# RWKV6 attention followed by an MLP on one core: the second MLP product of one more round in three one-pass products, with a new order of the work

## The chip, the cores and the metric

The kernel runs on one core of a Trainium2 chip. The metric is the device time in microseconds from launch to end, given as the median of several runs; a profile of one further execution shows where the time goes. TensorE (PE) does matrix products, VectorE (DVE), ScalarE (ACT) and GpSimd (POOL) do elementwise work, and SyncE (SP) issues nearly all DMAs.

## The reference

Inputs r, k, v, w are (4, 8, 768, 48) in fp32, u is (8, 48). The attention is a recurrence over 768 steps with a 48 x 48 state per batch and head:

```
for t in range(S):
    cur = einsum('bhd,bhe->bhde', u * kt, vt)
    y[:, :, t] = einsum('bhd,bhde->bhe', rt, state + cur)
    state = wt[:, :, :, None] * state + einsum('bhd,bhe->bhde', kt, vt)
```

Its output is laid out as x of (4, 768, 384), and the MLP block follows, with w_ch1 of (384, 1536) and w_ch2 of (1536, 384):

```
xn = (x - mu) / sqrt(var + 1e-06) * g_ln
out = x + maximum(xn @ w_ch1, 0) @ w_ch2
```

## The kernel before

**Rounds.** The work is cut into eight rounds: four batches by two halves of 384 steps. A round has a *front* (the attention) and a *back* (normalisation and MLP).

**Front.** Inputs are loaded (`nat_w`, `nat_k`, `nat_r`, `v`), multiplied up inside groups of four steps (`inner`), transposed on PE (`k_ps`, `r_ps`, `w_ps`) and copied out by ACT. The steps of a chunk of 64 are then combined over doubling distances: at each level PE multiplies r with k (`quads`, `a<-r,k` in the profile), and DVE scales k and r by products of w (`grow`, the in-place products `k<-k,tot` and `r<-r,tot`). When k is fully scaled, PE transposes it back (`kn_ps`), forms key-value products (`a<-v,k`), and DVE runs the state over the chunks (`s`, `last`). PE adds the part inside a chunk (`a<-v,A`) and the part from the state (`a<-s,r`), and x is copied out.

**Back.** DVE takes statistics (`stats`, `mv`), xn is made and transposed (`xT_ps`, `xf`). The first product has 12 blocks f of 128 hidden columns. In round 0 it is done in plain fp32, where one matmul goes through the array several times (two records in the profile). In rounds 1 to 7 (`THREE = 1`) xn and w_ch1 are split into a high part H, a low part L and a mixed part D, stored as fp32r, and three one-pass products give the same sum: `go_d` with D, a scaling in place by ACT (`shrink`), then `go` with L and H. H is made by ACT, L by DVE or POOL, D by DVE. The D part of w_ch1 lies in DRAM and is streamed in blocks (`d<-w1d`) into 32 homes.

**Second product.** There are two forms, and the number `LAST` decides. Rounds below `LAST` use plain fp32: for each of three tiles of 128 steps, 12 matmuls of 128 x 384 into one bank (`o<-ffn,h`), issued three at a time, and one DVE addition into x. Rounds from `LAST` on use `thirds`: ACT makes the H part of each h block, DVE or POOL the L part, DVE the D part, and for each f and tile three one-pass matmuls follow. The outputs lie in the two `a` banks (tiles 0 and 1) and in `o_2P` and `o_2D` (tile 2); two DVE additions per tile, scaled by `rstd` and `rstdD`, bring them into x, and each tile is stored by itself. Before, `LAST = NR - 4`, so rounds 4 to 7 use `thirds`.

**Where the parts of w_ch2 lie.** `halve2` makes the H, L and D parts of the second weight once. They go into the homes that the fronts use for k, r, A, nat_k, nat_r, v, vx and tot (`w2_place`). They can be written only when the last front no longer needs those homes; besides, the first matmul of a `thirds` round names x of the last round as needed:

```
if first:
    need += x_of(NR - 1)
```

So x of every round from `LAST` on is kept until then. Tile x has three homes, the last round's x lies in the home of `nat_w`.

**The order.** Each piece of work is an operation of the class `Plan` with a cost, what it needs, and the homes it takes. The table `ORDER` lists the operations in the order in which they are recorded; an entry above 10000 names the second or third engine where there is a choice. Each engine runs its instructions in that order. Where the planner expects PE to wait over 0.35 us it puts *fillers* in front, matmuls of zeros named `idle`, which write a free bank. All instructions are recorded by one helper, so every row of the profile has line 47, and tiles are the way to tell them apart.

Of the kernel before, what the change touches and what calls it, by code (L numbers as in the profile page):

```python
# [63 lines left out]
class Plan:  # L64
# [12 lines left out]
        2, 3, 10, 5, 14, 4, 12, 13, 8, 9, 265, 11, 16, 263, 260, 7, 18, 17, 19, 10015, 22, 10020, 264,  # L77
        10021, 25, 262, 27, 261, 23, 6, 24, 29, 266, 269, 267, 110, 268, 26, 128, 30, 270, 273, 271, 28,
        275, 112, 113, 42, 111, 272, 36, 122, 130, 276, 281, 98, 282, 283, 129, 131, 124, 10277, 278,
        65, 37, 38, 288, 274, 132, 43, 44, 10292, 10031, 123, 284, 289, 290, 286, 134, 35, 457, 279,  # L80
        291, 99, 45, 463, 287, 133, 10285, 140, 460, 39, 46, 47, 48, 49, 303, 32, 280, 136, 125, 50,
        10293, 126, 10053, 135, 100, 102, 306, 114, 305, 101, 464, 459, 127, 304, 458, 307, 297, 465,
        462, 461, 310, 308, 51, 311, 309, 10033, 312, 52, 103, 10034, 316, 54, 10294, 152, 313, 317,
        137, 296, 41, 142, 143, 433, 314, 315, 318, 411, 57, 60, 468, 55, 58, 63, 141, 59, 10323, 319,
        320, 116, 299, 321, 322, 56, 138, 466, 467, 139, 298, 470, 324, 327, 64, 69, 40, 70, 325, 469,
        10471, 10295, 330, 92, 66, 62, 61, 67, 117, 118, 68, 73, 328, 332, 473, 326, 104, 119, 329, 333,
        331, 475, 120, 338, 476, 71, 105, 340, 472, 72, 74, 75, 106, 78, 76, 77, 107, 79, 339, 10477,
        336, 344, 337, 10080, 81, 82, 300, 342, 0, 10085, 1, 482, 302, 301, 88, 90, 483, 10478, 91, 334,
        10474, 484, 146, 335, 345, 341, 89, 343, 485, 94, 86, 492, 488, 10095, 121, 144, 115, 87, 486,
        494, 493, 346, 347, 652, 348, 350, 349, 489, 154, 495, 353, 487, 490, 244, 246, 10496, 351, 93,  # L90
        354, 479, 242, 355, 158, 352, 153, 491, 145, 10497, 148, 147, 357, 356, 10498, 509, 10155, 358,
        243, 245, 10361, 247, 10362, 481, 510, 511, 248, 654, 164, 655, 365, 367, 96, 480, 156, 108,
        434, 249, 159, 366, 160, 149, 252, 250, 368, 109, 176, 363, 157, 97, 150, 162, 251, 364, 513,
        383, 658, 165, 653, 10161, 182, 413, 163, 384, 178, 166, 375, 167, 253, 240, 381, 373, 382, 236,
        10179, 177, 657, 376, 656, 183, 515, 514, 151, 516, 414, 660, 212, 369, 662, 241, 517, 435, 184,
        237, 10666, 659, 421, 664, 512, 663, 180, 214, 370, 425, 200, 501, 518, 500, 502, 503, 374, 387,
        10520, 385, 519, 170, 661, 521, 377, 254, 668, 171, 522, 504, 172, 173, 174, 386, 665, 378, 379,
        536, 505, 215, 506, 534, 168, 255, 670, 388, 185, 669, 532, 10499, 10671, 674, 258, 188, 535,
        533, 259, 10672, 850, 530, 528, 531, 10673, 10419, 380, 507, 256, 202, 10667, 83, 540, 213, 541,
        257, 529, 508, 524, 423, 389, 437, 201, 679, 391, 390, 537, 206, 525, 194, 675, 683, 424, 181,  # L100
        680, 527, 526, 449, 189, 676, 392, 10429, 238, 239, 684, 681, 538, 542, 371, 687, 203, 539, 677,
        682, 196, 847, 10439, 192, 543, 523, 10197, 689, 544, 169, 175, 412, 216, 218, 195, 372, 546,
        545, 198, 224, 547, 549, 436, 199, 688, 685, 204, 853, 851, 359, 550, 190, 551, 686, 690, 409,
        548, 220, 678, 10191, 186, 230, 207, 422, 205, 849, 426, 187, 193, 698, 552, 696, 697, 852, 417,
        410, 431, 210, 554, 360, 403, 10691, 398, 430, 219, 208, 225, 232, 848, 854, 695, 553, 222, 427,
        418, 555, 221, 10559, 209, 226, 704, 10233, 84, 707, 399, 706, 705, 228, 857, 404, 211, 393,
        855, 420, 699, 708, 441, 709, 10560, 231, 10558, 415, 217, 566, 234, 235, 710, 692, 856, 858,
        567, 394, 571, 428, 701, 416, 227, 229, 223, 10693, 700, 442, 572, 556, 395, 568, 712, 714, 573,
        10715, 859, 574, 432, 400, 557, 561, 562, 576, 405, 694, 713, 861, 401, 711, 10863, 406, 716,
        396, 703, 402, 575, 438, 601, 586, 591, 563, 860, 569, 564, 450, 443, 565, 570, 602, 407, 603,  # L110
        10864, 592, 440, 577, 578, 593, 397, 702, 717, 604, 447, 579, 723, 869, 720, 605, 580, 722,
        10865, 587, 725, 594, 724, 588, 726, 866, 731, 581, 870, 867, 10868, 595, 589, 727, 874, 582,
        721, 728, 732, 876, 590, 719, 871, 718, 729, 444, 10862, 877, 737, 596, 611, 448, 583, 730, 875,
        733, 872, 10455, 882, 597, 606, 738, 1045, 873, 883, 598, 1042, 584, 878, 880, 734, 1048, 445,
        881, 879, 599, 10453, 585, 607, 884, 735, 1047, 616, 1044, 741, 446, 646, 451, 608, 885, 742,
        736, 617, 10743, 600, 612, 456, 1043, 1050, 1049, 739, 452, 740, 10886, 899, 744, 618, 1046,
        901, 613, 10745, 1053, 1052, 900, 10746, 747, 1054, 619, 620, 454, 1055, 609, 614, 615, 11051,
        647, 903, 621, 748, 626, 622, 610, 1058, 890, 631, 1056, 636, 623, 11057, 893, 811, 891, 892,
        627, 887, 749, 904, 1060, 750, 1061, 905, 624, 816, 637, 625, 902, 10888, 894, 628, 632, 771,
        896, 638, 907, 10754, 1059, 633, 895, 1064, 10755, 634, 635, 909, 11062, 910, 906, 629, 648,  # L120
        908, 911, 1069, 776, 926, 1066, 630, 649, 1065, 753, 766, 1070, 639, 1063, 898, 912, 408, 650,
        922, 767, 768, 924, 917, 923, 806, 1071, 756, 925, 897, 757, 640, 10769, 1228, 1222, 1077, 1078,
        751, 641, 1072, 1073, 761, 1075, 762, 758, 1076, 914, 10759, 10889, 642, 1074, 1225, 763, 916,
        920, 1223, 1088, 1229, 918, 921, 643, 1226, 1230, 913, 770, 919, 10764, 1067, 644, 1085, 796,
        765, 760, 915, 1079, 1224, 777, 927, 1068, 1086, 1227, 1232, 645, 1231, 11236, 11237, 812, 1087,
        826, 1080, 807, 813, 1234, 778, 808, 928, 929, 781, 1094, 809, 814, 1096, 1097, 1233, 1095, 810,
        797, 11081, 1238, 1235, 11240, 798, 815, 779, 817, 930, 1098, 782, 786, 791, 799, 1101, 780,
        818, 783, 784, 787, 934, 788, 1100, 1089, 931, 1239, 932, 801, 789, 935, 11241, 11082, 790,
        1244, 819, 827, 11242, 933, 821, 939, 820, 936, 800, 1246, 828, 785, 1249, 792, 829, 802, 1091,
        1243, 10937, 1245, 1099, 1320, 1121, 1323, 1090, 10938, 1250, 830, 793, 1317, 1102, 1253, 1083,  # L130
        1084, 10940, 1092, 772, 794, 941, 1254, 1322, 1265, 803, 773, 795, 1103, 1319, 942, 1266, 944,
        1251, 804, 943, 1104, 1255, 1252, 1105, 1256, 1001, 1318, 1106, 1259, 1247, 1260, 1108, 1107,
        1109, 1325, 774, 822, 1093, 805, 945, 1257, 775, 1267, 1321, 1324, 1248, 823, 946, 1119, 1115,
        1268, 824, 1258, 966, 1269, 1326, 1327, 948, 1116, 1120, 825, 10949, 11329, 1122, 981, 950,
        1021, 1112, 1328, 1331, 11333, 836, 1334, 651, 1110, 1111, 1117, 1113, 1114, 831, 1123, 1274,
        1275, 752, 951, 952, 1330, 953, 1118, 832, 837, 1124, 11335, 961, 956, 1261, 957, 838, 841,
        11336, 839, 958, 842, 1276, 959, 1277, 954, 1339, 962, 11337, 1127, 1125, 1128, 1131, 1344, 843,
        833, 1338, 1332, 1341, 1340, 960, 1132, 1126, 11133, 1272, 1129, 1271, 1278, 1130, 1134, 840,
        11135, 1412, 1360, 1418, 1352, 1415, 971, 834, 955, 963, 1270, 1353, 1136, 10964, 1346, 835,
        1262, 1279, 965, 1345, 1419, 1280, 844, 1413, 1011, 1022, 1016, 1350, 1347, 1351, 1282, 1263,  # L140
        1416, 1362, 1301, 1414, 845, 1420, 1354, 1012, 1137, 1138, 1139, 1355, 947, 1285, 1281, 1284,
        1283, 1002, 1013, 1417, 1348, 1423, 1003, 1023, 1349, 1014, 1024, 1025, 982, 1015, 1004, 967,
        1017, 1286, 11422, 11424, 1005, 11425, 11421, 986, 991, 1302, 1273, 1369, 1006, 1207, 996, 1363,
        1140, 1018, 983, 1287, 1428, 1288, 1141, 1290, 1264, 1426, 1019, 1361, 1372, 976, 1289, 968,
# [1676 lines left out]
```

## Time and profile before

| | |
|---|---|
| median of 3 runs | 476.72 us (476.5 to 477.76) |
| the profiled execution, its own time | 480.65 us |
| its span, first to last instruction | 478.9 us |
| mean granted TensorE clock | 0.991 |
| DMA: moved, mean rate | 56.22 MB, 117 GB/s |

In the profile a row of a group gives the operation, output and inputs by the program's names (buffer numbers left out), sizes, the count, the busy time, the mean length of one, and the idle time in front of it with what ended it. PEld is the weight load, which overlaps the matmuls. A matmul's record is longer than its distance to the next one, since they are pipelined: the distance is what counts in a sum. The granted clock is 1.00 at full speed.

### The profile page before, as it was taken

Reading aid. Unit: us, or ns where it says so; the run is one execution under the profiler, and the core shown is the slowest. Engines: PE = TensorE matmul, PEld = TensorE weight load, DVE = VectorE, ACT = ScalarE, POOL = GpSimd, SP = SyncE. Lnnn points to the kernel's source line nnn. Section 1 sums busy time; section 2 is a strip of 40 time slices with the busy share of each in tenths; the row PEclk is TensorE's granted clock in tenths of the full one; section 3 lists DMA queues with packets and bytes.
Section 4 is the critical chain, followed back from the end, with each engine's and each line's share of the span. In section 5 each row is a group of like instructions: output and inputs, shape, how many; then the busy total and the mean of one; then the engine's idle time right before and its main releaser. Section 6 shows DMA issues by size and latency. Waiting matters only on the chain. (4 is left out here: it accounts for less than half of the span.)

```text
span 478.9 us, 17278 instructions
## 1 busy us (share of the span) xinstructions
PE 465.8 (97%) x7390; PEld 396.4 (83%) x7390; DVE 349.1 (73%) x734; ACT 259.6 (54%) x595; POOL 117.2 (24%) x125
## 2 busy tenths in 40 slices
PE   8998999999989999999999999999999999999996
PEld 4667989766878778996679986779999999999996
DVE  6999999999938766895957986793986543533454
ACT  6786889653842255364215664357683764453530
POOL 3126019013601213603315201000342122102012
PEclk9999999999997999999999999999999999999999
DMA  7985685677265463276186125116231221341001
GB/s 213 262 212 133 196 182 159 187 175 182 70 185 125 117 177 89 65 161 163 23 214 174 25 54 108 30 50 164 83 102 38 86 73 35 103 129 35 26 24 66
DMA packets 105468, 56.22 MB, mean 117 GB/s; under 512 B 61872, under 2 KB 102320, under 8 KB 105392
## 3 DMA queue, kind: packets, MB, share of 16 engines
q1 hardware_dynamic: 105120, 54.92, 44.3%
q8 instruction: 58, 0.95, 0.8%
q14 instruction: 18, 0.15, 0.1%
q10 hardware_dynamic: 272, 0.20, 0.1%
HBM read 45.27 MB, written 7.47 MB: 110 GB/s over the span
## 5 line engine op out<-in xcount | busy, mean ns | idle before, releaser
L47 PE MATMUL o<-ffn,h 128*128 128x384 f32 x288 | 99.8, 489 | 0.0
L47 ACT ACTIVATE h<-h_ps 128x384 f32<-128x384 f32 (+2 forms) x108 | 47.2, 454 | 64.1 <-PE h_ps L47 61.0
L47 PEld LDWEIGHTS o<-ffn,h 128*128 128x128 f32 x288 | 52.3, 190 | 29.1 <-issue 0.2
L47 ACT ACTIVATE h_ps<-h_ps 128x384 f32<-128x384 f32 x84 | 39.1, 478 | 36.6 <-PE h_ps L47 35.7
L47 DVE SCALAR_TENSOR_TENSOR hD<-hH,hL 128x384 fp32r<-128x384 f32 x48 | 26.5, 569 | 35.9 <-POOL hL L47 16.6
L47 PEld LDWEIGHTS a<-r,k 48*56 48x56 f32 (+3 forms) x3072 | 40.1, 123 | 11.9 <-issue 5.8
L47 PE MATMUL h_ps<-xd,d 128*128 128x384 f32 x204 | 48.2, 343 | 0.0
L47 PE MATMUL a<-r,k 48*56 48x32 f32 (+3 forms) x3072 | 44.2, 209 | 3.0 <-issue 2.1
L47 POOL TENSOR_TENSOR hL<-h,hH 128x384 fp32r<-128x384 f32 x22 | 26.2, 1198 | 82.5 <-PE o_2D L47 21.3
L47 PE MATMUL h_ps<-xhl,wl 128*128 128x384 f32 x180 | 42.7, 347 | 0.0
L47 PE MATMUL h_ps<-xhl,wh 128*128 128x384 f32 x180 | 40.1, 333 | 0.0
L47 DVE TENSOR_TENSOR r<-r,tot 112x768 f32<-112x768 f32 (+1 forms) x40 | 32.2, 808 | 9.5 <-PE a L47 9.5
L47 PEld LDWEIGHTS h_ps<-xd,d 128*128 128x128 f32 x204 | 34.3, 189 | 2.7 <-issue 0.3
L47 DVE TENSOR_TENSOR k<-k,tot 112x768 f32<-112x768 f32 (+1 forms) x40 | 31.5, 790 | 6.5 <-PE a L47 5.8
L47 PEld LDWEIGHTS h_ps<-xhl,wh 128*128 128x128 f32 x180 | 31.8, 194 | 0.0
L47 PEld LDWEIGHTS h_ps<-xhl,wl 128*128 128x128 f32 x180 | 31.0, 196 | 0.9 <-ACT h_ps L47 0.2
L47 ACT COPY A<-a 32x384 f32<-32x384 f32 (+5 forms) x60 | 25.0, 424 | 11.3 <-PE a L47 7.1
L47 ACT ACTIVATE hH<-h 128x384 fp32r<-128x384 f32 x48 | 24.1, 518 | 12.4 <-PE a L47 8.7
L47 ACT ACTIVATE xf<-xT_ps,g_sb 128x384 f32<-128x384 f32 (+2 forms) x27 | 14.6, 545 | 24.1 <-PE xT_ps L47 22.3
L47 PE MATMUL h_ps<-xf,w 128*128 128x128 f32 (+1 forms) x144 | 26.2, 332 | 0.0
L47 PE MATMUL idle<-nought 128*128 128x384 f32 (+2 forms) x74 | 24.5, 455 | 0.9 <-DVE eps L47 0.9
L47 DVE TENSOR_TENSOR hL<-h,hH 128x384 fp32r<-128x384 f32 x26 | 14.9, 585 | 14.0 <-PE o_2P L47 5.7
(183 smaller groups left out, 1071.0 us busy)
## 6 DMA issues: line engine op xcount, KB each, us to landing
d<-w1d SPq DMA_DIRECT2D x84, 192.0 KB, 3.0
raw<-in_moe_w_ch_dram SPq DMA_DIRECT2D x24, 384.0 KB, 4.3
nat_w<-in_w_dram SPq DMA_DIRECT2D x24, 192.0 KB, 3.7
nat_r<-in_r_dram SPq DMA_DIRECT2D x24, 192.0 KB, 3.8
v<-in_v_dram SPq DMA_DIRECT2D x24, 192.0 KB, 4.3
nat_k<-in_k_dram SPq DMA_DIRECT2D x23, 192.0 KB, 4.0
w1d<-w1diff SPq DMA_DIRECT2D x12, 192.0 KB, 3.4
out_dram<-x SPq DMA_DIRECT2D x4, 576.0 KB, 4.2
```

The source lines that it names most:

```text
L47: ins = self.tc.keep_in_program_order(f(*args, **kw))
```

## The change

Two numbers and a table change. `LAST` becomes `NR - 5`, so rounds 3 to 7 have their second product as `thirds`, and only rounds 0 to 2 in plain fp32. Rounds above `LAST` put the split parts of xn by turns into two sets of homes (`x_places`), and which round uses which set shifts by one. Tile x gets a fourth home. `ORDER` is replaced as a whole: 2,190 entries instead of 2,124, in a different order from the first entry on, with different choices between DVE, ACT and POOL. The order was searched under random instruction fetches.

```diff
     ORDER = [
-        2, 3, 10, 5, 14, 4, 12, 13, 8, 9, 265, 11, 16, 263, 260, 7, 18, 17, 19, 10015, 22, 10020, 264,
+        10008, 3, 2, 10012, 4, 9, 10, 5, 11, 16, 264, 261, 7, 14, 13, 18, 10019, 262, 17, 265, 260, 263,
...
     HOMES = {
         "nw": 1, "nk": 1, "nr": 1, "pk": 1, "pr": 1, "w4": 1, "vals": 2, "va": 2,
         "k": 2, "r": 2, "tot": 1, "decay": 3, "rk": 1,
-        "v": 1, "vx": 1, "s": 2, "last": 3, "x": 3, "xn": 3,
+        "v": 1, "vx": 1, "s": 2, "last": 3, "x": 4, "xn": 3,
...
     BY = {"DVE": DVE, "POOL": POOL}
     EITHER = ("DVE", "POOL")
-    THREE, LAST = 1, NR - 4
+    THREE, LAST = 1, NR - 5
```

In instructions, 36 plain fp32 matmuls of 128 x 384 go and 108 one-pass matmuls come; DVE has 742 instructions instead of 734, ACT 608 instead of 595, POOL 141 instead of 125, SP 316 instead of 314. The fillers are 45 instead of 37. The first matmul of a second product in one-pass form stood behind 3,728 matmuls of the program and now stands behind 3,589; the first hD stood behind 608 DVE instructions and now stands behind 581.

252 rows, old and new, of the table ORDER are left out of this document.

## The prediction

> **What bounds the kernel now.** I began with the totals on the page of the profile, then cut the span into stretches with the busy time of each engine, then read the groups by cost. The total says that TensorE (PE) is nearly always busy and no other engine comes close:
>
> ```profile
> span 478.9 us, 17278 instructions
> PE 465.8 (97%) x7390; PEld 396.4 (83%) x7390; DVE 349.1 (73%) x734; ACT 259.6 (54%) x595; POOL 117.2 (24%) x125
> ```
>
> An average over stages can hide a second limit, so here is busy time by stretch. The columns are the stretch, its length, then PE, PEld, DVE, ACT and POOL with their counts, the granted clock and the DMA share:
>
> ```profile
> 0.00:50.00 50.00, 45.03 (x812) 32.44 (x813) 46.23 (x121) 38.13 (x87) 16.16 (x33) 1.00 0.75 198
> 50.00:120.00 70.00, 69.98 (x1327) 54.92 (x1326) 68.87 (x136) 48.80 (x120) 19.53 (x16) 1.00 0.71 184
> 120.00:140.00 20.00, 18.89 (x351) 16.79 (x351) 14.23 (x36) 13.71 (x32) 7.79 (x7) 1.00 0.51 144
> 140.00:150.00 10.00, 8.63 (x149) 8.31 (x141) 5.93 (x9) 1.77 (x4) 2.00 (x3) 0.66 0.41 105
> 150.00:348.00 198.00, 197.69 (x4004) 160.41 (x4003) 148.83 (x309) 96.10 (x215) 44.19 (x44) 1.00 0.44 106
> 348.00:474.00 126.00, 125.21 (x770) 123.48 (x769) 63.16 (x124) 61.04 (x142) 27.48 (x23) 1.00 0.20 61
> ```
>
> Three regimes stand here. Up to 120 us VectorE (DVE) is full, 46.23 of 50 and then 68.87 of 70 us, and PE is kept going beside it. From 150 to 348 us PE alone is full (197.69 of 198) and DVE has a quarter of its time free. From 348 us on, the one-pass second products of rounds 4 to 7 run, and PE is full again while DVE works half the time. From about 50 us on, then, work taken off PE shortens the kernel, as long as DVE can deliver sooner what PE needs.
>
> **The main term: the second product of round 3.** The old form is timed where 24 records of it stand in a row (two records make one matmul), up to the start of the next instruction; the new form where 18 one-pass matmuls do in the chain that ended last:
>
> ```profile
> 228.12 7.91 PE L47 MATMUL o<-ffn,h 128*128 128x384 f32 x24
> 235.96 0.25 PE L47 MATMUL a<-v,A 64*64 64x48 f32 x1
> ```
>
> ```profile
> 468.06 2.92 PE a L47 x18
> 470.99 0.16 PE o_2D L47
> ```
>
> Twelve old matmuls take 235.96 - 228.12 = 7.84 us, 0.653 each; 36 of them make a round, 23.5 us. One new matmul takes (470.99 - 468.06) / 18 = 0.163 us; a round has 12 x 3 x 3 = 108, 17.5 us (the mean group rows are longer since neighbouring records overlap). The term is -6.0 us. The weight loads stay hidden: in the stretch from 348 us they run 123.48 of 126 us beside matmuls that lose only 0.79. If that cover went, the price would be bounded by the same 0.79 of 126 us, under 0.2 us for this round.
>
> **What the new form adds on other engines.** Twelve times a high, a low and a difference part of h, six additions into x instead of three, and three stores instead of one:
>
> ```profile
> L47 DVE SCALAR_TENSOR_TENSOR hD<-hH,hL 128x384 fp32r<-128x384 f32 x48 | 26.5, 569 | 35.9 <-POOL hL L47 16.6 <-PE a L47 10.6 <-PE o_2P L47 6.4
> L47 POOL TENSOR_TENSOR hL<-h,hH 128x384 fp32r<-128x384 f32 x22 | 26.2, 1198 | 82.5 <-PE o_2D L47 21.3 <-PE h_ps L47 17.6 <-ACT h_ps L47 10.2
> L47 ACT ACTIVATE hH<-h 128x384 fp32r<-128x384 f32 x48 | 24.1, 518 | 12.4 <-PE a L47 8.7 <-PE o_2D L47 1.5 <-PE o_2P L47 1.3
> L47 DVE TENSOR_TENSOR hL<-h,hH 128x384 fp32r<-128x384 f32 x26 | 14.9, 585 | 14.0 <-PE o_2P L47 5.7 <-ACT hH L47 3.9 <-issue 1.8
> L47 DVE SCALAR_TENSOR_TENSOR x<-a,rstdD,x 128x384 f32<-128x384 f32 x8 | 4.8, 613 | 8.1 <-PE a L47 8.1
> ```
>
> The order gives DVE 12 more hD (12 x 0.569 = 6.8 us), 6 more hL (6 x 0.585 = 3.5) and three more additions (3 x 0.613 = 1.8): 12.1 us. POOL gets 6 hL (6 x 1.198 = 7.2) and ACT 12 hH (12 x 0.518 = 6.2). All of it falls in the last regime, where DVE is busy 63.16, ACT 61.04 and POOL 27.48 of 126 us, so I cost it at nothing. The three smaller stores of round 3 go to SP's queue; behind a store that waits for its addition stand later loads of weight pieces, which have 32 homes to run ahead in, so this too is nothing. The last additions and stores of round 7 are unchanged, and so is the tail.
>
> **What moves.** The parts of the second weight can be made only when every front is done, because they lie in the fronts' homes. Round 3's second product therefore leaves the middle and joins the last regime. On PE, in the middle of the program before, four-pass triples (o3 is round 3's output tile) fill time between pieces of the fronts of rounds 6 and 7:
>
> ```order
> L47 MATMUL a0_66<-r6_4071,k6_4038 32x32 x48
> L47 MATMUL o3_2_4630<-ffn2_6_1439,h3_6_4431 128x384
> L47 MATMUL o3_2_4630<-ffn2_7_1700,h3_7_4251 128x384
> L47 MATMUL o3_2_4630<-ffn2_8_1413,h3_8_4642 128x384
> L47 MATMUL o3_0_4832<-ffn2_3_1146,h3_3_4377 128x384
> L47 MATMUL o3_0_4832<-ffn2_4_1474,h3_4_4395 128x384
> L47 MATMUL o3_0_4832<-ffn2_5_1612,h3_5_4659 128x384
> L47 MATMUL k_ps7_1_4922<-ident_80,pad_k_71 112x128 x4
> L47 MATMUL r_ps7_2_4927<-ident_80,pad_r_72 112x128 x4
> ```
>
> On PE after, the first such work stands behind all fronts, next to round 4's first product (a0 and a1 are output banks, the letter in w2D and hD names the part):
>
> ```order
> L47 MATMUL h_ps4_1_5622<-xk4_4982,wh0_1_1218 128x384
> L47 MATMUL h_ps4_1_5622<-xr4_4983,wh0_2_1037 128x384
> L47 MATMUL a0_66<-w2D0_5340,hD3_0_5606 128x384
> L47 MATMUL a0_66<-w2L0_5334,hL3_0_5491 128x384
> L47 MATMUL a0_66<-w2H0_4969,hH3_0_5263 128x384
> L47 MATMUL a1_67<-w2D0_5340,hD3_0_5606 128x384
> L47 MATMUL a1_67<-w2L0_5334,hL3_0_5491 128x384
> L47 MATMUL a1_67<-w2H0_4969,hH3_0_5263 128x384
> ```
>
> Counting ahead of the first hD matmul: the 36 old matmuls are gone (-23.5 us) and so is a round's worth of first-product matmuls (129 of rounds 4 and 5 before, 21 after: 108 x 0.163 = 17.5 us). PE has 41 us less to fill the front with. DVE loses less there: 581 instructions ahead of its first hD instead of 608. At the 150 to 348 us stretch's mean, 148.83 / 309 = 0.48 us, that is 13 us. So the middle asks DVE for 148.8 - 13.0 = 135.8 us of work in 198 - 41 + 3.5 (next term) = 160.5 us, a share of 85% instead of 75%. Between 50 and 120 us it runs at 98% while PE misses 0.02 us, so 85% can be done; but each place where PE waits for DVE has a shorter cover. The nearest row for such a wait:
>
> ```profile
> PE kn_ps L47 <- DVE k L47: 1.1, 1, 1.1
> ```
>
> Bounds: nothing, since at 98% PE lost nothing, and several such waits, 6 us or more (the second rival). I take one, +1.1 us. The fourth home for x eases one thing: the first outputs of round 6 need the home of round 2 instead of round 3, whose product ends much earlier; I cost it at nothing, as no row shows a wait for it.
>
> **The opening.** On PE at the end of the opening before, the last fillers (idle matmuls, put where the planner expects PE to wait) stand ahead of round 0's first transposes of xn:
>
> ```order
> L47 MATMUL kn_ps0_1_0_697<-ident_80,k0_211 128x112 x4
> L47 MATMUL idle_702<-nought_76 128x384
> L47 MATMUL idle_702<-nought_76 128x128
> L47 MATMUL a0_66<-v0_258,k0_211 48x48 x16
> L47 MATMUL a1_67<-v0_258,k0_211 48x48 x16
> L47 MATMUL w_ps1_0_748<-ident_80,w4_73 112x128 x3
> L47 MATMUL idle_754<-nought_76 128x128
> L47 MATMUL xT_ps0_1_0_756<-ident_80,xn0_0_745 128x128
> ```
>
> On PE after, fillers stand on both sides of those transposes, up to the first first-product matmul:
>
> ```order
> L47 MATMUL idle_896<-nought_76 128x128
> L47 MATMUL xT_ps0_2_0_898<-ident_80,xn0_0_891 128x128
> L47 MATMUL w_ps1_0_903<-ident_80,w4_73 112x128 x3
> L47 MATMUL k_ps1_1_907<-ident_80,pad_k_71 112x128 x4
> L47 MATMUL xT_ps0_0_0_919<-ident_80,xn0_0_891 128x128
> L47 MATMUL xT_ps0_1_0_921<-ident_80,xn0_0_891 128x128
> L47 MATMUL a0_66<-s1_647,r0_210 64x48 x16
> L47 MATMUL idle_943<-nought_76 128x128
> L47 MATMUL a1_67<-r1_802,k1_872 60x32 x48
> L47 MATMUL h_ps0_3_0_995<-xf0_0_941,w1_1_0_107 128x128
> ```
>
> In all there are 45 fillers instead of 37, with 12,416 columns instead of 10,368, and the single filler that stood in the middle is gone.
>
> ```profile
> L47 PE MATMUL idle<-nought 128*128 128x384 f32 (+2 forms) x74 | 24.5, 455 | 0.9 <-DVE eps L47 0.9
> ```
>
> At that row's 24.5 us for 10,368 columns, 2,048 more cost 4.8 us; at the 0.653 us per 384 columns of the warm rows, 3.5 us; if they only fill waits that PE has anyway, nothing. What is not done while DVE paces the opening must be done later on a full PE, so I take +3.5 us.
>
> **A stall and a slow clock.** The stretch 140 to 150 us has a mean granted clock of 0.66. Finer, with the PE instruction at its start:
>
> ```profile
> 141.93 1.30 PE L47 MATMUL a<-r,k 48*60 48x32 f32 x49 [1.37 <-issue]
> ...
> 140.00:142.00 2.00, 0.63 (x44) 0.52 (x39) 0.00 (x0) 0.00 (x0) 0.59 (x2) 1.00 0.19 52
> 142.00:144.00 2.00, 2.00 (x86) 2.00 (x88) 0.63 (x1) 0.67 (x1) 0.00 (x0) 0.55 0.07 20
> 144.00:146.00 2.00, 2.00 (x18) 1.91 (x13) 1.79 (x4) 0.00 (x0) 0.00 (x0) 0.50 0.61 192
> 146.00:148.00 2.00, 2.00 (x8) 2.00 (x7) 1.97 (x4) 1.05 (x2) 0.36 (x1) 0.50 0.65 143
> 148.00:150.00 2.00, 2.00 (x9) 1.88 (x9) 1.53 (x3) 0.05 (x1) 1.05 (x1) 0.74 0.53 118
> ```
>
> PE stands for 1.37 us amid small matmuls and waits for nothing that the profile shows (issue), and then its clock is down over the four stretches of 2 us that follow: 2 x (0.45 + 0.50 + 0.50 + 0.26) = 3.4 us lost. Together 4.8 us. The order after puts other instructions at every such place, so the pair may be gone (-4.8), stay (0) or come twice (+4.8). I take half of its going, -2.4 us, because the plain runs have a median 3.9 us under the profiled one and may not have it each time.
>
> The Trainium skill, page "TensorE: Matmul & The Clock Gate", section "Why this matters for your kernels", says that the clock drops after idle gaps above about 3 us between matmul bursts. By that rule a gap of 1.4 us would cost only itself, the term would be half of 1.4, and the sum below -2.1 instead of -3.8. The trace differs: here 1.37 us among small matmuls was enough.
>
> **The sum.** -6.0 + 3.5 + 1.1 - 2.4 = -3.8 us. The profiled execution takes 480.65 us (span 478.9 and 1.75 around it) and would take 476.9. The shown runs have a median of 476.72; the same difference gives 472.9. About 0.3%, 1.43 us, is what a measurement of this kernel can tell from no change.
>
> **The rivals.**
>
> Nothing left over: the saving is eaten where DVE paces the kernel. The opening costs 4.8 us, plain runs never had the slow clock, and one wait on DVE stays: -6.0 + 4.8 + 1.1 = -0.1 us, 476.6. For it: DVE is full in the opening and the fillers were raised by a fifth. Against: PE's saving is certain work, and most fillers lie where PE waits anyway. Chance 0.20.
>
> Slower: DVE becomes the bound of the middle. The place is the transposes of k (kn_ps) and the quads of rounds 4 to 7, which wait for DVE's scaling of k and r, with 41 us less filler beside them. If DVE gets only to 80% there, halfway between today's 75 and the needed 85, its 135.8 us take 169.8 instead of 160.5: +9.3. In place of the 1.1 the sum is -4.9 + 9.3 = +4.4, 481.1. It decides (1.43 us slower) from 6.3 us of loss, a share of 135.8 / 166.8 = 81%. For it: the order after gives POOL more work, 141 instructions instead of 125, and DVE instructions are seen at twice their length:
>
> ```profile
> L47 DVE SCALAR_TENSOR_TENSOR hD<-hH,hL x48: 523/557/1300, 348.0 to 470.1; 128x384 fp32r<-128x384 f32 x48
> ```
>
> Against: the 98% above. Chance 0.20. The Trainium skill, "GPSIMD Engine Reference", section "Specifications", says that POOL shares its SBUF interfaces with VectorE and contends with DVE instructions that have two SBUF inputs. By that rule POOL's middle work of 44.19 us, grown as 141 to 125, would put 5.7 us more on DVE and lift its share from 85 to 88%, which speaks for this rival and is still below 98%.
>
> More than forecast: the opening's fillers cost nothing net, and the pair of stall and clock was in the plain runs and goes: -6.0 - 4.8 + 1.1 = -9.7; with half of the fillers' 3.5 it is -8.0, 468.7. Chance 0.08.
>
> **The numbers.** The forecast has the rest, 0.52, with a range of its own from 470.5 to 475.3 (-6.2 where the pair of stall and clock goes for good, -1.4 where nothing of it goes). Faster: 0.52 + 0.08 = 0.60; within 0.3%: 0.20; slower: 0.20. The range leaves out half of the case of more and half of the slower case: 468.5 to 481.0.
>
> **What would show it.** Right: round 3's second product as 108 matmuls 0.163 us apart; the first hD near 348 - 37.5 = 310 us; PE without idle time from about 60 us to its end; DVE near 85% in the middle; no granted clock below 1.0 behind the opening. Wrong: idle time of PE put down to DVE k or r in rounds 4 to 7, or first real PE work several us later than before, or a new slow stretch of the clock.

## The result, and the profile after

| | before | after |
|---|---|---|
| median | 476.75 us | 469.45 us (469.27 to 469.62, 4 runs) |
| profiled execution, its own time | 480.65 us | 469.36 us |
| its span | 478.9 us | 467.6 us |
| mean granted clock | 0.991 | 1.0 |

The ratio of after to before is 0.9841, with an interval from 0.9828 to 0.9855: 7.3 us less, where the forecast was 3.8 less. After was timed only here; beside the experiments before was timed again, with medians from 476.38 to 476.79 us, so differences of under half a microsecond below say nothing. One execution of before (586.06 us at a mean granted clock of 0.753) and one of the changed kernel with two pieces in experiments 8 to 12 (488.19 us at 0.943; without it the median there is 475.17 us) were in a slower state. The totals of the changed kernel:

```profile
span 467.6 us, 17460 instructions
PE 459.7 (98%) x7442; PEld 400.8 (86%) x7442; DVE 352.5 (75%) x742; ACT 264.5 (57%) x608; POOL 139.1 (30%) x141
```

Busy time by stretch, with the columns as before (PE, PEld, DVE, ACT, POOL, granted clock, DMA share, GB/s). The fifth row is the middle, cut at 309 us where the one-pass second products take over:

```profile
0.00:50.00 50.00, 47.68 (x835) 34.05 (x839) 47.52 (x126) 36.60 (x85) 21.02 (x30) 1.00 0.84 225
50.00:120.00 70.00, 69.34 (x1326) 54.97 (x1318) 66.86 (x132) 49.82 (x122) 18.42 (x18) 1.00 0.70 176
120.00:140.00 20.00, 20.00 (x429) 18.81 (x428) 19.05 (x43) 15.38 (x36) 10.51 (x8) 1.00 0.60 164
140.00:150.00 10.00, 10.00 (x239) 9.43 (x233) 8.04 (x15) 5.33 (x12) 1.79 (x4) 1.00 0.75 156
150.00:309.00 159.00, 158.47 (x3711) 130.34 (x3703) 132.99 (x281) 81.13 (x183) 54.12 (x51) 1.00 0.46 107
309.00:463.00 154.00, 154.00 (x954) 153.17 (x952) 76.49 (x147) 76.22 (x172) 33.27 (x31) 1.00 0.22 66
```

PE is full from 120 us on but for 0.5 us, the clock is 1.00 in every row, and in the middle DVE has 132.99 of 159 us, 84%. In the opening PE stands idle for 2.32 of 50 us where before it was 4.97. The groups that answer to those of before, and the row of hD with its minimum, median and maximum and its first and last start:

```profile
L47 DVE SCALAR_TENSOR_TENSOR hD<-hH,hL x60: 526/558/1390, 300.9 to 458.5; 128x384 fp32r<-128x384 f32 x60
...
L47 PE MATMUL idle<-nought 128*128 128x384 f32 (+2 forms) x90 | 29.6, 452 | 0.9 <-DVE eps L47 0.9
```

The one-pass second product keeps its price, nine matmuls in 1.46 us (0.162 each) in the chain that ended last:

```profile
459.32 1.46 PE a L47 x9
```

What PE still waits for, by what ended the wait (total, times, longest):

```profile
PE idle L47 <- DVE eps L47: 0.9, 1, 0.9
PE a L47 <- issue: 0.9, 2, 0.7
PE k_ps L47 <- POOL pad_k L47: 0.6, 1, 0.6
PE a L47 <- DVE hD L47: 0.4, 1, 0.4
PE a L47 <- DVE s L47: 0.3, 1, 0.3
PE a L47 <- ACT r L47: 0.2, 1, 0.2
```

These are 3.3 us in all. To see what they were, a run of the old order is needed without the stall and the slow clock that stood at 140 us in the profile of before. The first experiment happens to be that.

### The profile page after: what moved, and what is told of

The parts are those of the page before. It is cut to its first block, busy times and chain, and to the rows that moved or that the text cites. A ratio compares the mean times of both kernels' runs of the same rounds, so it can differ in the third digit from the quotient of the medians.

```text
span 467.6 us, 17460 instructions
## 1 busy us (share of the span) xinstructions
PE 459.7 (98%) x7442; PEld 400.8 (86%) x7442; DVE 352.5 (75%) x742; ACT 264.5 (57%) x608; POOL 139.1 (30%) x141
## 4 chain that ended last, share of the span: by engine, by line
PE 86%; DVE 6%; DMA 3%; ACT 2%; POOL 2%; issue 1%; DVEq 0%; SPq 0%; POOLq 0%; ACTq 0%
PE h_ps L47 28%; PE a L47 25%; PE o L47 15%; PE o_2P L47 4%; PE idle L47 3%; PE r_ps L47 2%; PE k_ps L47 2%; PE o_2D L47 2%; DMA raw<-in_moe_w_ch_dram 2%; PE kn_ps L47 2%; PE xT_ps L47 2%; DVE s L47 1%; ACT held L47 1%; DMA va<-own_d 1%; POOL nat_k L47 1%
## 5 line engine op out<-in xcount | busy, mean ns | idle before, releaser
L47 PE MATMUL o<-ffn,h 128*128 128x384 f32 x216 | 74.6, 491 | 0.0
L47 DVE SCALAR_TENSOR_TENSOR hD<-hH,hL 128x384 fp32r<-128x384 f32 x60 | 36.4, 617 | 37.1 <-POOL hL L47 16.0
L47 POOL TENSOR_TENSOR hL<-h,hH 128x384 fp32r<-128x384 f32 x28 | 30.2, 1084 | 102.7 <-PE a L47 27.7
L47 PEld LDWEIGHTS o<-ffn,h 128*128 128x128 f32 x216 | 39.2, 190 | 23.0
L47 PE MATMUL h_ps<-xhl,wl 128*128 128x384 f32 x180 | 40.4, 334 | 0.0
L47 DVE TENSOR_TENSOR k<-k,tot 112x768 f32<-112x768 f32 (+1 forms) x40 | 31.6, 791 | 6.7 <-PE a L47 4.7
L47 ACT ACTIVATE hH<-h 128x384 fp32r<-128x384 f32 x60 | 29.7, 519 | 11.6 <-PE a L47 7.8
L47 DVE TENSOR_TENSOR hL<-h,hH 128x384 fp32r<-128x384 f32 x32 | 18.0, 569 | 20.0 <-PE a L47 9.5
L47 PE MATMUL idle<-nought 128*128 128x384 f32 (+2 forms) x90 | 29.6, 452 | 0.9 <-DVE eps L47 0.9
L47 ACT COPY A<-a 32x384 f32<-32x384 f32 (+5 forms) x56 | 23.6, 422 | 11.9 <-DVE xhl L47 5.6
L47 PE MATMUL a<-w2D,hD 128*128 128x384 f32 x90 | 29.7, 330 | 0.4 <-DVE hD L47 0.4
```

The costliest lines, as they stand in the source:

```text
L47: ins = self.tc.keep_in_program_order(f(*args, **kw))
```

## Experiment 1: the fourth home of x alone

The kernel before, with one number of the change:

```diff
-        "v": 1, "vx": 1, "s": 2, "last": 3, "x": 3, "xn": 3,
+        "v": 1, "vx": 1, "s": 2, "last": 3, "x": 4, "xn": 3,
```

> The kernel before with a fourth home for x and nothing else. Theory (the home only makes the fifth round possible): 476.75 us, within 0.5. Rival (the home takes a wait away by itself): under 475.3.

Measured: 476.38 us, ratio to before 0.9995 (0.9986 to 1.0004). The home alone does nothing. Its profile has a span of 474.4 us, and the stretch in which the profile of before had a clock of 0.50 reads:

```profile
142.00:144.00 2.00, 2.00 (x36) 1.95 (x29) 2.00 (x4) 0.94 (x2) 0.00 (x0) 1.00 0.03 10
144.00:146.00 2.00, 2.00 (x12) 1.81 (x11) 1.97 (x4) 1.10 (x3) 0.17 (x1) 1.00 0.81 215
146.00:148.00 2.00, 2.00 (x47) 1.12 (x47) 1.54 (x3) 0.56 (x2) 1.23 (x1) 1.00 0.65 185
```

The instructions and their order are those of before, the clock is 1.00, and the time is the plain median. So the pair of stall and slow clock belongs to the profiled execution of 480.65 us and not to the median. It is not the only such execution: of 64 others of before, run beside the experiments, nine took 478.1 to 482.5 us, at mean granted clocks of 0.991 to 0.996. The median has nothing of them, so the pair's going can't be part of the 7.3 us. This profile is the right one to hold after against. What PE waits for in it:

```profile
PE kn_ps L47 <- DVE k L47: 1.1, 1, 1.1
PE a L47 <- DVE last L47: 1.1, 2, 0.7
PE idle L47 <- DVE eps L47: 0.9, 1, 0.9
PE w_ps L47 <- POOL w L47: 0.8, 1, 0.8
PE a L47 <- DVE hD L47: 0.8, 2, 0.5
PE a L47 <- DVE s L47: 0.7, 1, 0.7
PE a L47 <- DVE r L47: 0.4, 2, 0.3
PE w_ps L47 <- DVE w L47: 0.3, 1, 0.3
PE k_ps L47 <- POOL pad_k L47: 0.3, 1, 0.3
PE a L47 <- DVE k L47: 0.2, 1, 0.2
PE a L47 <- issue: 0.2, 1, 0.2
PE a L47 <- POOL token L47: 0.2, 1, 0.2
PE xT_ps L47 <- ACT xn L47: 0.2, 1, 0.2
```

They sum to 7.2 us, against 3.3 after: 3.9 less. The same can be had from PE's records, if each is counted from its start to the start of the next one, so that a wait counts to the instruction ahead of it:

| PE's time, us | before, profiled | x: 4 alone | after |
|---|---|---|---|
| both MLP products | 324.2 | 321.7 | 313.8 |
| fronts, transposes of xn | 123.9 | 121.0 | 119.4 |
| fillers | 25.3 | 26.3 | 29.0 |
| last PE record ends at | 474.4 | 470.0 | 463.2 |

From the second column to the third it is -7.9 - 1.6 + 2.7 = -6.8 us, and that is also what the spans say (467.6 - 474.4). These times hold the waits. With each wait taken out of the row in which it is counted, the products fall by 6.4 us, the fronts by 0.6, the fillers grow by 4.1, and the waits are the 3.9 less.

## Experiment 2: one more pass for round 3

The changed kernel, in which the L pass of round 3's second product runs twice: 36 more one-pass matmuls, four passes instead of three. The output counts that part twice.

```diff
-                    to, tiles[L_][:, ts(i, P)], mixed(w2_part("L", f)), start=first, stop=False
+                    to, tiles[L_][:, ts(i, P)], mixed(w2_part("L", f)), start=first and rnd != 3, stop=False
...
             def both(i=i):
                 go_d(i)
+                if rnd == 3:
+                    PE.matmul(
+                        as_pairs(out_tiles(i)[0]), tiles[L_][:, ts(i, P)], mixed(w2_part("L", f)),
+                        start=first, stop=False,
+                    )
```

> The changed kernel with the L pass of round 3's second product done twice (36 one-pass matmuls more, four passes in all, as many as fp32 takes; its output counts that part twice). Nothing else moves. Theory (PE is the bound and the saved pass is worth its own time): 469.45 + 36 x 0.163 = 475.3 us, within 0.7. Rival (the new order alone brought the gain, and PE has slack where the passes now stand): under 471.

Measured: 475.77 us, ratio to before 0.9984 (0.9958 to 1.001), with runs from 474.38 to 480.49; span 472.6, that is 5.0 above after; the medians differ by 6.3. At 0.163 us each, 36 matmuls are 5.9 us, and PE's records of these products, waits taken out, grow by 5.8. In that stretch a pass costs what it takes, and with four passes in round 3 almost nothing is left of the change. That is the arithmetic of the main term read backwards: the fp32 form spends four one-pass times (0.653 against 4 x 0.163 = 0.652), so the saving of the change is one pass in four, 36 x 0.163 = 5.9 us.

## Experiments 3 and 4: are the fillers lost time?

In the first, all fillers but the first run keep their number and place and are cut to 8 columns; in the second, to half of their columns.

```diff
...
-                t[:, 0 : now * P], zeros, nought.broadcast_to([P, now * P]), start=True, stop=True
+            wide = 8 if filled else now * P
+            PE.matmul(t[:, 0:wide], zeros, nought.broadcast_to([P, wide]), start=True, stop=True)
```

> The changed kernel with all fillers but the first run cut from up to 384 columns to 8, their number and every place unchanged. The first run is 8 matmuls of the 45; the rest take about 22 us of the group's 29.6. The prediction put 3.5 us on eight more fillers, as if their time were lost. Theory A (fillers only stand where PE waits anyway): within 1 us of 469.45. Theory B (filler time delays real work, as the term of +3.5 supposed): 3 to 10 us faster. Theory C (they keep the clock up): slower, with a granted clock of 0.5 to 0.7 in the opening, 472 or more.

> The changed kernel with all fillers but the first run at half their columns (192 for 384), number and places unchanged; with 8 columns the clock fell to 0.5 from 12 to 50 us and the kernel was 4.4 us slower. Theory A (what keeps the clock up is PE busy for most of each stretch, and the fillers are near the least that does it): the clock falls again in part of the opening, 0.5 to 0.8, and the time is 470 to 474. Theory B (there is more filler than needed, and its surplus delays real work): clock 1.0 and 1 to 3 us faster than 469.45.

Measured: 473.88 us with 8 columns, 4.4 above after, and 470.33 with half, 0.9 above. The stretches with 8 columns:

```profile
10.00:20.00 10.00, 7.74 (x101) 7.02 (x101) 9.91 (x21) 6.50 (x15) 0.69 (x2) 0.66 0.95 274
20.00:30.00 10.00, 8.85 (x245) 8.20 (x245) 8.10 (x25) 6.47 (x17) 0.91 (x1) 0.65 0.80 206
30.00:40.00 10.00, 10.00 (x166) 9.48 (x165) 9.08 (x23) 9.55 (x24) 6.34 (x2) 0.50 0.69 135
40.00:50.00 10.00, 10.00 (x155) 9.19 (x158) 9.18 (x29) 5.13 (x15) 6.21 (x8) 0.50 0.73 213
```

And with half of them:

```profile
20.00:30.00 10.00, 9.79 (x274) 8.68 (x266) 8.51 (x26) 6.61 (x18) 0.84 (x1) 0.63 0.83 220
30.00:40.00 10.00, 10.00 (x161) 8.76 (x162) 9.94 (x22) 9.35 (x23) 7.67 (x4) 0.68 0.85 177
```

Theory C of the first and theory A of the second held. The fillers hold the clock: without their width it is 0.50 for 20 us, and the front's own matmuls grow into the freed time (PE is busy 10.00 of 10 us there, at half speed). The time freed is small besides: waits taken out, PE's time in fillers falls only from 27.9 to 21.6 us. Yet a clock that is down by a third over 20 us costs only 0.9 us (in the trace it is 0.50 from 22.7 to 36.3 us and 1.00 around that): DVE is busy 8.51 and 9.94 of 10 us in these rows, and PE's slower matmuls largely fit in beside it. So a filler's duration is neither lost nor free. The prediction's price, duration times number, counts what would otherwise be plain waiting or a slower clock.

## Experiments 5 to 7: how near is DVE to being the bound of the middle?

A reduction, whose result is not used, behind each of the 32 scalings of k and r in rounds 4 to 7: 128 x 640 (0.81 us each, 25.9 us together) in the changed kernel and in the kernel before, and 128 x 256 (0.41 us, 13 us together) in the changed one. The edit below is the wider one; the other has 2 in place of 5.

```diff
...
+            if 4 <= rnd <= 7:
+                DVE.tensor_reduce(
+                    out=spare, in_=ident[:, None].broadcast_to([P, 5, P]), axis=AX.XY, op=ALU.max
+                )
```

> The changed kernel with a reduction of 640 columns added on DVE behind each of the 32 scalings of k and r in rounds 4 to 7, some 0.74 us each, 24 us of DVE time in the middle, where DVE is busy 133.0 of 159 us; its result is not used. Theory A (the middle has 26 us of free DVE time that can be had): 0 to 6 us slower. Theory B (the rival by which DVE becomes the bound: the scalings stand on the path and the spare time lies in the wrong places): each added reduction shows on PE, 12 to 24 us slower, with PE waiting for DVE k, r or last.

> The changed kernel with a reduction of 256 columns behind each of the 32 scalings of rounds 4 to 7, about 0.4 us each, 13 us of DVE time in the middle instead of the 25.9 that cost 9.1 us. Theory A (DVE has free time in the middle up to a knee, and the 25.9 went past it): the middle asks 133 + 13 = 146 of 159 us, 92%; 0 to 2.5 us slower, less than half of 9.1. Theory B (each one delays PE by its share, 35% of its length, wherever DVE's load stands): 4.5 us slower, 474.

> The kernel before with the same 32 reductions of 640 columns, 25.9 us. Theory A (the middle of the kernel before holds 49 us of free DVE time, 148.8 of 198, with PE work beside it): 0 to 3 us slower than before, 476.7 to 479.7, with few waits of PE for DVE. Theory B (the scalings stand on the path, and anything put behind them is late by its length in either kernel): 8 to 10 us slower, as in the changed kernel, 485.

| | DVE added | time | against its own kernel |
|---|---|---|---|
| changed kernel | 13 us | 471.76 us | +2.3 |
| changed kernel | 25.9 us | 478.51 us | +9.1 |
| kernel before | 25.9 us | 489.77 us | +13.0 (+13.2 by the 476.53 of its own comparison) |

With 25.9 us the changed kernel lies between its two theories. With 13 it is where theory A put it, and the two together show a bend: the first 13 us cost 2.3, the next 13 cost 6.8. The middle of the two runs, the smaller one first:

```profile
150.00:309.00 159.00, 156.61 (x3645) 127.41 (x3635) 142.72 (x309) 80.96 (x183) 52.08 (x51) 1.00 0.46 107
```

```profile
150.00:309.00 159.00, 150.58 (x3582) 120.87 (x3582) 148.62 (x298) 75.44 (x171) 49.97 (x49) 1.00 0.44 103
```

PE misses 2.4 and 8.4 us of its 159, at DVE shares of 90% and 93%. The change stands at 84%. Three points do not say where between 84% and 93% the bend lies.

The third run overturned theory A, and with it a part of my reasoning; it lies above theory B's 8 to 10 us too. The middle of the kernel before has twice the free DVE time and loses more. Its stretch:

```profile
150.00:362.00 212.00, 203.88 (x3931) 165.56 (x3930) 176.13 (x346) 100.01 (x223) 45.91 (x46) 0.98 0.43 104
```

DVE has 36 us free there, a share of 83%, and still PE misses 8.1 us. One wait stands out in the row of time (start, length, and in brackets the idle time ahead and who ended it), and the clock behind it:

```profile
274.13 2.46 PE L47 MATMUL a<-r,k 48*56 48x32 f32 x96 [2.31 <-DVE r L47]
...
274.00:276.00 2.00, 1.87 (x80) 1.87 (x84) 1.82 (x5) 0.00 (x0) 0.78 (x1) 0.50 0.00 0
276.00:278.00 2.00, 2.00 (x78) 1.91 (x71) 1.34 (x2) 0.00 (x0) 1.78 (x2) 0.50 0.03 8
278.00:280.00 2.00, 2.00 (x8) 2.00 (x8) 2.00 (x7) 0.00 (x0) 0.00 (x0) 0.50 0.02 4
```

A wait of 2.31 us, and then half speed to 280.8 us, 6.8 us in all by the trace, which is 3.4 us more. How much free time DVE has over a stretch does not say what a late scaling costs. That what the order lets PE do meanwhile decides it is my reading, and no run isolates it. Shown is that the new order, with less work to fill in, bears the same lateness better, by 3.9 us, about as much as that one slow clock.

## Experiments 8 to 12: the place of the instructions

The change's words speak of random instruction fetches, and the profile of before had a stall that nothing in it explains (issue). The trace has 58 transfers of the instruction queue:

```profile
q8 instruction: 58, 0.95, 0.9%
```

With 7,442 PE records and as many weight loads these are about 257 instructions to a transfer. The Trainium skill, page "Runtime: NRT & Kernel Launch", section "Instruction fetch mechanics", gives 256 instructions to a block of 16 KiB, which agrees, and calls the crossing mostly hidden.

First I shifted all PE instructions of both kernels by 60 or so, with 16 tiny fillers in the first run of fillers:

```diff
...
+        if first:
+            n -= 16 // 8
+            for _ in range(16):
+                PE.matmul(t[:, 0:8], zeros, nought.broadcast_to([P, 8]), start=True, stop=True)
```

> The changed kernel with the same shift. Theory (its order is less open to such a fetch, wherever it falls): within 1.4 us of 469.45, no slow clock. Rival (the changed kernel was only lucky in where its fetches fall): 471 to 474, with a stall and a slow clock in the profile.

> The kernel before with 16 tiny matmuls of zeros added to the first filler (and as much taken off it), so that every later PE instruction stands 56 to 64 places further on and the blocks in which PE's instructions are fetched begin elsewhere; order and work are the same. Theory (the stall at 140 us with its slow clock is a fetch of instructions that falls among small matmuls): the pair moves or goes, and the time differs from 476.75 by over 1.4 us, down to 472 or up to 481. Rival (the stall has another cause): the pair stays near 140 us and the time is within 0.7 of 476.75.

Measured: 484.65 us, 15.2 above after, and 485.81 us, 9.1 above before (ratio 1.0181, 1.0159 to 1.0203). My theory that the changed kernel would not mind fell, and the loss is beyond the rival's 471 to 474 too. In the kernel before no wait is left near 140 us, but experiment 1 has none there either, so that says nothing, and 485.81 is above the 481 that the theory allowed. And both runs have a fault of their own, seen in the first rows of the changed kernel's trace:

```profile
0.93 14.26 PE L47 MATMUL idle<-nought 128*128 128x8 f32 x46 [0.93 <-DVE eps L47]
15.03 0.60 PE L47 MATMUL k_ps<-ident,pad_k 128*112 128x128 f32 x4
```

The first transpose, at 9.03 us after the change, starts at 15.03: the 32 records of 8 columns stand 0.213 us apart, and 6 of the 15 us may be that late start. So the shift was made again where it takes little time (0.2 us with two pieces and 0.8 with three, by PE's records of these matmuls): 32 of the 36 fp32 matmuls of round 0's second product, near 100 us, are cut into two of 192 columns (64 PE records more, half a transfer), or, as the control, into three of 128 (128 records more, one whole transfer).

```diff
...
+                        c = RN // 2 if rnd == 0 and f_ * TT + i > 3 else RN
+                        for q in range(0, RN, c):
                             PE.matmul(
-                            tiles[o], tiles[f"h{rnd}_{f_}"][:, ts(i, P)], tiles[f"ffn2_{f_}"],
-                            start=f_ == 0, stop=f_ == FC - 1,
+                                tiles[o][:, q : q + c], tiles[f"h{rnd}_{f_}"][:, ts(i, P)],
+                                tiles[f"ffn2_{f_}"][:, q : q + c],
+                                start=f_ == 0, stop=f_ == FC - 1 and q + c == RN,
                             )
```

> The changed kernel with 32 of the 36 fp32 matmuls of round 0's second product cut into two of 192 columns: the same columns, 32 matmuls more, and every later PE instruction stands 64 records (128 instructions with their weight loads) further back. The trace has 58 transfers of the instruction queue of 16 KB each for 2 x 7442 PE instructions, 257 to a transfer, so this moves the later program by half a transfer. Theory A (where the transfers cut the program decides whether stretches of small matmuls stall): new waits put down to issue with a granted clock of 0.5 behind them, behind 90 us; 473 to 479 us, as the run with 16 tiny fillers lost 15 us of which only 6 were its own late start. Theory B (that run lost by its late start and what followed from it): within 1.4 us of 469.45.

> The control of the former: the same 32 matmuls cut into three of 128 columns, so that later PE instructions stand 256 places further back, one whole transfer of the instruction queue by 2 x 7442 / 58 = 257. Theory A: the transfers cut the later program where they do in the changed kernel, but for a place or so, no new stall behind round 1; within 1.4 us of 469.45, and several us below the kernel with two pieces. Theory B: both alike. If it is as slow as with two pieces or slower while that one is slow too, the cutting itself costs and A is not shown.

> The kernel before with the same 32 matmuls of round 0's second product cut into two of 192 columns, so that every later PE instruction stands half a transfer of the instruction queue further back. In the changed kernel this cost 5.8 us, and 1.4 us with a whole transfer. Theory A (an order fits one position of the transfers, and both orders were made with it): 2 to 8 us slower than before, 478.5 to 484.5, with waits put down to issue behind 115 us. Theory B (only the new order sits close to a stall): within 1.4 us of before.

| | time | against its own kernel |
|---|---|---|
| changed kernel, half a transfer | 475.23 us (472.78 to 488.19) | +5.8 |
| changed kernel, a whole transfer | 470.85 us (470.08 to 475.8) | +1.4 |
| kernel before, half a transfer | 482.64 us (482.0 to 486.1) | +5.9 |

Theory A held in its times and its waits. Its slow clock did not show in the profiled execution of the changed kernel with two pieces (473.96 us, 1.00 behind the start), though eight others had mean granted clocks of 0.995 or 0.996 and took 474.6 to 476.3 us. The control, just at the bound it was given, has more of the cutting and less of the loss, so in the new order it is the position that costs. For the old order no control was run; there the waits must say it. Half a transfer off, those put down to issue are:

```profile
142.59 0.67 PE L47 MATMUL a<-s,r 48*64 48x48 f32 x26 [0.86 <-issue]
187.66 0.65 PE L47 MATMUL h_ps<-xhl,wh 128*128 128x384 f32 x3 [1.28 <-issue]
260.45 0.53 PE L47 MATMUL a<-r,k 48*60 48x32 f32 x24 [1.54 <-issue]
308.77 0.29 PE L47 MATMUL a<-v,k 64*48 64x48 f32 x5 [1.16 <-issue]
```

These are 4.8 us, where experiment 1 has 0.2. The new order has no such wait behind 52 us; half a transfer off, its longest is

```profile
284.23 0.32 PE L47 MATMUL a<-s,r 48*64 48x48 f32 x5 [1.70 <-issue]
```

and the control has 0.48 us at that place. In the run with two pieces the issue waits come to 3.5 us, in the control to 2.1, and another 1.3 us is a wait for `last`. All of these rows but one stand among small matmuls, and that one, of h_ps, was stopped 1.7 us behind 144 of them. In the kernel before with tiny fillers, 96 of those took 1.41 us, so 128 records go by in 1.9 us, where 128 one-pass matmuls of 0.163 take 20.9 us:

```profile
243.67 1.41 PE L47 MATMUL a<-r,k 48*56 48x32 f32 x96
...
248.89 0.68 PE L47 MATMUL a<-s,r 48*64 48x48 f32 x15 [3.34 <-issue]
```

The traces also hold the time of each transfer of the instruction queue, and they can be laid beside the four waits of the old order:

| PE goes on at | it stood for | transfer begun | landed | from landing to PE's going on |
|---|---|---|---|---|
| 142.59 us | 0.86 us | 140.28 us | 141.15 us | 1.4 us |
| 187.66 us | 1.28 us | 184.60 us | 186.22 us | 1.4 us |
| 260.45 us | 1.54 us | 258.04 us | 258.98 us | 1.5 us |
| 308.77 us | 1.16 us | 306.54 us | 307.48 us | 1.3 us |

In all fourteen traces 37 of PE's waits are put down to issue, and 36 of them end 1.1 to 1.7 us behind the landing of such a transfer (the other one, of 0.8 us, is in the changed kernel with 25.9 us of reductions). PE's other waits keep no such distance: they end from 1.4 us ahead of a landing to 22 us behind one. So it is shown that in these waits PE stands until its next instructions are there. Why they are late is not shown by itself; an estimate from these numbers is that a block comes too slowly for small matmuls, since from a transfer's start to PE's going on it is 2.2 us at the least, and they use up a block in 1.9. Most crossings are hidden, as that page of the Trainium skill has it: the trace of after has a wait put down to issue behind 2 of its 58 transfers, the old order half a transfer off behind 4. Half a transfer costs either order about 6 us. But the position does not explain the change's gain: with nothing shifted such waits come to 0.2 us in experiment 1 and 0.9 after.

## Why the prediction was right

The direction and the range held, and the time came out 3.5 us below the forecast. By its own steps:

- **The main term, -6.0 us: right.** PE's time in the products fell by 6.4 us, waits taken out (experiment 1). The pass removed from round 3 is worth its own duration (experiment 2: 5.0 by the spans, 6.3 by the medians, for one pass). The work that it adds on DVE, ACT and POOL is hidden, as costed: PE is full, 154.00 of 154 us, from 309 us on.
- **The opening, +3.5 us: too dear, for want of a term.** The fillers' own time, waits taken out, grew by 4.5 us in the opening, within the bounds, and the single filler in the middle gave 0.4 back. But the fillers replace plain waits. In the list of waits of experiment 1, those for `last` (1.1 us), POOL w (0.8), s (0.7), r (0.4), DVE w (0.3), `pad_k` (0.3), DVE k (0.2) and xn (0.2) all lie ahead of 47 us, 4.0 us with the last one here:

```profile
46.42 0.25 PE L47 MATMUL a<-v,A 64*64 64x48 f32 x1 [0.72 <-DVE last L47]
```

  After, `pad_k` (0.6), s (0.3) and r (0.2, from ACT) are left of them, and 0.9 us of issue, the greater part at 51 us, has come: 2.0 us together. That is 2.0 us back, and the opening cost +2.5: by 60 us PE has done 31.6 us of work other than fillers in experiment 1 and 29.1 after. With the 0.4 it is +2.1. The prediction's sentence that what is not done in the opening must be done later is borne out; what it left out is the waits that go. Experiments 3 and 4 show that a filler's duration is not its price.
- **One more wait for DVE in the middle, +1.1 us: the wrong sign.** The share came as worked out (84%, forecast 85), and no wait came with it. The one that there was, kn_ps for k at 1.1 us, went, one of 0.2 for POOL's token too, and those for hD, in the last regime, fell from 0.8 to 0.4: -1.6 us. The step that failed is "each place where PE waits for DVE has a shorter cover". Cover is what the order puts at a place and not the total; the new order bears late scalings better (experiment 7), though why is argued.
- **The stall and the slow clock, -2.4 us: not there.** The median never had the pair (experiment 1; such executions are nine of 64). The prediction had seen the hint, a median 3.9 us under the profiled execution, and took half. The median was the evidence, and the term should have been 0.
- **The sum:** -6.4 for the products, +2.1, -1.6, and -0.8 for fronts and one small wait that no term had: -6.7 us, where the spans of experiment 1 and after differ by 6.8 and the medians by 6.9 (7.3 from before's own). The forecast's -3.8 was right in direction since its main term was; of its smaller terms two were too high, by 1.4 and 2.7 us, and one too low by 2.4, so that errors partly cancelled. The range from 468.5 to 481.0 is wide, and 469.45 lies 1 us from its lower end.
- **The rivals.** "Nothing left over" counted fillers at 4.8 us, of which 2.1 was lost, and kept a wait that went. "DVE becomes the bound" had the right place and the wrong distance: it needs some 13 us more on DVE before it costs over 2 us. "More than forecast" came nearest in time, 468.7, with half of the fillers' price; but its other half, the pair that goes, was not what happened, so that nearness is luck.
- **The signs.** The first hD starts at 300.9 us instead of 310: in the run of experiment 1 it starts at 343.6 and not 348.0, so 4.4 of the 9 us are the pair again. From 60 us to its end PE has one wait over 0.15 us, 0.4 us for hD. No clock below 1.00, no idle time for DVE k or r in rounds 4 to 7.
- **The two rules of the Trainium skill.** "TensorE: Matmul & The Clock Gate", section "Why this matters for your kernels", warns of idle gaps above about 3 us as what drops the clock. The runs bear out neither that as a bound nor my reading of one stall: 3.34 us was followed by half speed, 2.31 and 1.37 too, but 1.70 and 1.54 were not; behind one of 0.83 us in the changed kernel with tiny fillers it fell too, and with thin fillers at no wait above 1.4 us. What decides it stays open. "GPSIMD Engine Reference", section "Specifications", would have put more on DVE; POOL's busy time in the middle rose to 54.12 us in 159, and DVE's share came out below the forecast and not above.

What stays open: which part of the 3.9 us of waits that went is owed to round 3's product having left the middle, and which to the search for an order, since neither can be had without the other here.

## What to carry to other kernels

Take the sizes of a forecast from the plain median wherever one profiled execution shows something that the others need not have: a difference between the two is itself a reading. On an engine that is full, a removed pass is worth its own time, and what the move does to waits is a matter of the order at a few places, which shares of busy time don't show. Where an order is tuned to the position of its instructions, any edit ahead of a stretch of small matmuls can cost as much as the change brings, so compare it with a control that shifts by a whole block, and lay the waits that nothing explains beside the transfers of the instruction queue.

## What was not expected of the hardware

- Half a block of PE instructions more, near 100 us and without a column more, costs either order about 6 us (475.23 against 469.45, 482.64 against 476.75); a whole block costs the new order 1.4. PE's unexplained waits end 1.1 to 1.7 us behind the landing of an instruction transfer, 36 of 37.
- Fillers of 8 columns in a row take as long as fillers of 128: their records stand 0.11 us apart at a granted clock of 1.00, and 0.21 where it is 0.50, as those of 128 columns do. So 16 of them at the start of the program, with 256 columns less of other fillers in their place, delay the first transpose by 6.0 us.
- 20 us at a mean granted clock of 0.63 to 0.68 in the opening, where DVE is busy 8.51 and 9.94 of 10 us, went with a median only 0.9 us longer.
